# A planned kernel whose plan reckons loads at another rate, with one product issued in two pieces

## The chip, the cores and the metric

The kernel runs on one core of a Trainium2 chip. The core's engines work side by side, each through a list of instructions of its own, in order: TensorE (matrix products; PE in the profile, with its weight loads as PEld), VectorE (DVE), ScalarE (ACT), GpSimd (POOL) and SyncE (SP). In this kernel GpSimd does little but issue the loads from DRAM, and SyncE issues the transposes and the stores. An instruction that needs another engine's result waits for a semaphore, and everything behind it in its engine's list waits with it.

The metric is the time of one execution on the device in microseconds (us), as the median of several runs.

## The reference, cut to what matters

The inputs are u and v (8 sequences x 3072 tokens x 256), z (8 x 3072 x 64), and the weights w1, w2 (256 x 1024) and w_out (1024 x 256).

```python
scores = (1 / S) * z @ z.T            # per sequence, S = 3072
attn = max(scores, 0) ** 2
x = u * (attn @ v)                    # 24576 tokens x 256
h1, h2 = x @ w1, x @ w2
out = max(h1, h2) @ w_out
```

## The kernel before, in words

**The arithmetic.** max(h1, h2) is h2 + max(h1 - h2, 0). So the kernel forms w1 - w2 once, computes d = x (w1 - w2), takes its ReLU as g, and adds g @ w_out and x @ (w2 @ w_out). The product of w2 and w_out, called W2o, is made once, amid the first sequence: sixteen transposes of w2 on TensorE (job "w2t"), two copies of them out of PSUM to the tile w2T (jobs "w2T", 0 on VectorE and 1 on ScalarE), sixteen matrix products (job "w2o"), and two copies of the result to W2o_sb on ScalarE (jobs "w2o", 0 and 1). The two result tiles lie in two of the three pairs of PSUM banks that all score, d and output products share.

**Steps and groups.** A sequence has 24 blocks of 128 tokens, in six groups of four. A step works on one group of columns: 48 steps in all, six to a sequence. The score matrix is symmetric, so a tile of scores that one step has squared is transposed by a DMA (jobs "turn", issued by SyncE) and read again by a later step; a step's own diagonal tile is completed in the same way. The first three steps use plain products; the others use a seven-product scheme for 2 x 2 blocks, for which VectorE makes sums and differences of the score tiles (es), of the values v (the folds, lf) and of the accumulators (e). For each step TensorE does first products ("Xa", "Xb") and second products ("Ya", "Yb") into two accumulators, with the d products and output products of the steps before laid in between.

**The plan.** Nothing is scheduled by hand at the instruction level. The kernel declares jobs: what a job writes and reads, which jobs it needs, which engines can do it and at what reckoned cost. The order of TensorE is fixed by the list `work` (lines 1271 to 1380), into which the score tiles are laid. Then `find_orders` (line 1774) plays the jobs through, engine by engine: each engine takes, of the jobs that are ready by the reckoning, the one due first; ReLUs, squares and the like may go to ScalarE or VectorE. `find_dues` (line 1750) sets the due times from TensorE's list. `share_wide` (line 1851) gives the 19 wide buffers (score tiles, turned tiles, also w2 and w2T) to tiles by the reckoned end of their last use, and `share_mm` (line 1869) the pairs of PSUM banks. Up to 24 rounds are played, with a margin added to each job that TensorE had to wait for, and the round with the earliest reckoned end gives the order of every engine's list. On the chip only the lists, the buffers and the semaphores are left: the reckoned times are not enforced.

**How the plan reckons a DMA.** All DMAs of GpSimd and SyncE go through one line in `settle` (line 1789): `dma_free` is the time at which the line is free, and each DMA adds its own time, from the table `DMA`, times a factor: `DMA_FULL` = 1.1 for those that begin in the plan's first 100 us, `DMA_PART` = 0.9 later. SyncE also can't be more than 4.5 us ahead of that line (`DMA_AHEAD`). So in the plan a load makes the transposes behind it late, and the other way round. Loads that are timed start when TensorE reaches a given instruction (`load`, line 106).

Of the kernel before, what the change touches and what calls it, by code (L numbers as in the profile page):

```python
# [11 lines left out]
def kernel(  # L12
# [23 lines left out]
    B, S, D = u.shape  # L36
# [10 lines left out]
    KD = D // P  # L47
# [37 lines left out]
    def matmul(*args, **kw):  # L85
        newest[0] = pin(nc.tensor.matmul(*args, **kw)).ins  # L86
        for ins in fence:
            tc.add_manual_dep(newest[0], ins.name, SYNC, reason="a bank's other half of rows")
        fence.clear()
# [148 lines left out]
    def tile_of(pool, key):  # L238
        return bufs[pool, key].tile
# [1035 lines left out]
    def put(ns, shares, key, reads=()):  # L1275
        work.append((ns, shares, key, reads))
# [29 lines left out]
    for n, st in enumerate(steps):  # L1306
        if not st.plain:
            m = n - LAG + 1

            def d_part(part, i, m=m):  # L1310
                put(430, True, ("d" + part, m, i))

            def half(name, which, begin=lambda i: None, groups=slice(None)):
                for i, g in enumerate(st.groups[groups]):
                    begin(i)
                    put(
                        PE256 * (4 if which else 3),
                        False,
                        (name, n, g),
                        rows_read(st, g) if name == "Xa" else (),  # L1320
                    )

            seven = steps[n - LAG].seven

            def d_parts(names):
                for name in names.split():
                    d_part(name[0], int(name[1]))

            if n == LAG:
                put(900, True, ("w2t",))  # L1330
                put_d(0)
                half("Xa", 0, lambda i: put(1800, True, ("w2o",)) if i == W2O_AT else None)
            if seven:
                put_seven(n - LAG, 0)
                d_parts("a0")
                put_seven(n - LAG, 1)
                d_parts("b0")
            else:
                put_o(n - LAG)
            if n > LAG:  # L1340
                half("Xa", 0)
                if seven:
                    put_seven(n - LAG, 2)
                else:
                    d_parts("a0")
            half("Xb", 0)
            if seven:
                if n == LAG:
                    put_seven(n - LAG, 2)
                d_parts("a1 a2")  # L1350
                put_seven(n - LAG, 3)
                d_parts("b1 b2")
                half("Ya", 1, lambda i: d_parts("a3") if i == A3_AT else None)
            else:
                d_parts("b0 a1 a2 b1 b2 a3" if n > LAG else "a0 a1 b0 a2 b1 b2 a3")
                half("Ya", 1)
            d_parts("b3")
            half("Yb", 1)
            continue
        lat = LAT_OWN if n > LAG else 6 * 432  # L1360
        own = st.rows
        n_plain = 0

        def put_plain(ks, dcs, reads):
            global_i = len(plain_todo)
            i = sum(t[0] is st for t in plain_todo)
            plain_todo.append((st, i, ks, dcs))
            put(PE512 * len(ks) * len(dcs), False, ("plain", st.n, i), reads)

        for i, k0 in enumerate(own):  # L1370
            if i in ((0, 1) if n else ()) + (len(own) - 2, len(own) - 1):
                if i in (0, len(own) - 2):
                    ks = [own[i], own[i] + 1, own[i + 1], own[i + 1] + 1]
                    for dc in range(KD):
                        put_plain(ks, [dc], [((n, own[i]), lat), ((n, own[i + 1]), lat)])
                continue
            for k in (k0, k0 + 1):
                put_plain([k], range(KD), [((n, k0), lat)])
# [229 lines left out]
        after=at_step(0, 2, 6),  # L1608
    )

    def w2o_products(_):
        for dc in range(KD):
            ps = tile_of("mm", ("w2o", dc))
            for nb in range(KF):
                matmul(
                    ps[:, 0, :D],
                    tile_of(*W2T)[:, dc, nb, :],
                    w_out_sb[:, nb, :],
                    start=(nb == 0),
                    stop=(nb == KF - 1),  # L1620
                )

    job(
        ("w2o",),
        {"PE": 16 * PE256},
        w2o_products,
        deps=[("w2T", 0), ("w2T", 1), ("wo",)],
        new=[("mm", ("w2o", dc)) for dc in range(KD)],
        uses=[W2T],
        lag=150,  # L1630
    )
    for dc in range(KD):
        job(
            ("w2o", dc),
            {"ACT": 300},
            lambda eng, dc=dc: copy(eng, W2o_sb[:, dc, :], tile_of("mm", ("w2o", dc))[:, 0, :D]),
            deps=[("w2o",)],
            uses=[("mm", ("w2o", dc))],
            lag=200,
        )  # L1640
# [133 lines left out]
    def find_orders():  # L1774
        idle_from = {"PE": 0, "ACT": 900, "DVE": 1300, "SP": 0, "POOL": 0}
        ready = {e: [] for e in idle_from}
        emitted = []
        dma_free = [10000]

        def release(j):  # L1780
            at = 0
            for d in j.all_deps:
                at = max(at, d.done)
            for d in j.all_after:
                at = max(at, d.begin + 1)
            for e in j.ways:
                ready[e].append((at, j))

        def settle(j, begin, ns):
            j.begin, j.done = begin, begin + ns + j.lag  # L1790
            if j.key in FIRST_LOADS:
                j.done = FIRST_LOADS[j.key]
            elif j.dma:

                dma_free[0] = max(dma_free[0], begin + DMA_START["SP" if "SP" in j.ways else "POOL"]) + (DMA_FULL if begin < DMA_FULL_TO else DMA_PART) * j.dma
                j.done = dma_free[0] + DMA_END
                if "SP" in j.ways:
                    idle_from["SP"] = max(begin + SP_ISSUE, dma_free[0] - DMA_AHEAD)
            for nxt, _ in j.succ:
                nxt.waits -= 1  # L1800
                if not nxt.waits:
                    release(nxt)

        for j in list(jobs.values()):
            if not j.waits and j.key not in HEAD_JOBS:
                release(j)
        for key in [k for k in jobs if k in HEAD_JOBS]:
            settle(jobs[key], -1, 0)
            for e in jobs[key].ways:
                ready[e] = [r for r in ready[e] if r[1] is not jobs[key]]  # L1810


        def left_to_act(j, t):
            if j.key[0] not in ("relu", "g", "oc"):
                return False
            return max(t, idle_from["ACT"]) + j.ways["ACT"] <= max(t, idle_from["DVE"]) + j.ways["DVE"] + RELU_BIAS


        def left_to_dve(j, t):
            if j.key[0] != "square":  # L1820
                return False
            return max(t, idle_from["DVE"]) + j.ways["DVE"] <= max(t, idle_from["ACT"]) + j.ways["ACT"] + SQUARE_BIAS

        while len(emitted) < len(jobs) - len(HEAD_JOBS):
            best = None
            for e, todo in ready.items():
                if e == "DVE":
                    todo = [r for r in todo if not left_to_act(r[1], r[0])]
                if e == "ACT":
                    todo = [r for r in todo if not left_to_dve(r[1], r[0])]  # L1830
                if not todo:
                    continue
                found = [(max(t, idle_from[e]), j.due, j) for t, j in todo]
                at, _, j = min(found, key=lambda x: x[:2])

                if e != "PE":
                    near = [x for x in found if x[0] <= at + PATIENCE]
                    at, _, j = min(near, key=lambda x: x[1] + WAIT_COST * (x[0] - at))
                if best is None or at < best[0]:
                    best = at, e, j  # L1840
            assert best, [k for k, j in jobs.items() if j.begin is None][:20]
            at, e, j = best
            for o in j.ways:
                ready[o] = [r for r in ready[o] if r[1] is not j]
            idle_from[e] = at + (j.ways[e] if e != "POOL" else 1000)
            settle(j, at, j.ways[e])
            emitted.append((j, e))
        return emitted
# [149 lines left out]
```

## Time and profile before

| | us |
|---|---|
| median of 3 runs | 898.25 |
| lowest and highest of them | 895.57, 901.81 |
| the profiled execution | 892.38 |
| its span, first to last instruction | 890.3 |
| TensorE busy in the span | 883.2 |
| VectorE, ScalarE, GpSimd busy | 790.7, 757.8, 60.0 |

The profiled execution is one run of its own, so durations from it are set against 892.38, not against the median. A row of a group or of the timeline gives the start (in us from the span's start), the time taken, engine, line, operation and the tiles in the form out<-in; "x3" means three such instructions merged; what stands in brackets is the engine's idle time ahead of it and what ended it. A row of the windows gives, for a stretch, its length and then busy time and count of TensorE, its weight loads, VectorE, ScalarE and GpSimd, then the granted TensorE clock, the DMA engines' share and GB/s. A row of DMA issues ends with the us from issue to landing. Many operations of this kernel share a helper's line (L86 is every matrix product, L103 every DMA of SyncE, L107 every load), so tiles and order tell which is meant.

### The profile page before, as it was taken

What the parts mean: (1) busy time and instruction counts of PE and PEld (TensorE: products, weight loads), DVE (VectorE), ACT (ScalarE), POOL (GpSimd) and SP (SyncE); (2) the same over time, 40 slices, a digit from 0 to 9 for tenths busy, and PEclk for the clock granted to TensorE, in tenths of its full rate; (3) what the DMA queues carried; (4) which work ended last, traced back from release to release, by engine and by line L of the source; (5) the groups of instructions that cost most, each with busy time, mean ns of one, the idle gap of its engine ahead of it and who ended that gap; (6) DMA issues with size and microseconds to landing.
All of it is one profiled execution on the core that took longest, in us unless ns stands there. A gap on an engine that the chain in (4) does not pass through costs nothing.

```text
span 890.3 us, 37187 instructions
## 1 busy us (share of the span) xinstructions
PE 883.2 (99%) x16349; PEld 736.2 (83%) x16349; DVE 790.7 (89%) x1698; ACT 757.8 (85%) x951; POOL 60.0 (7%) x127
## 2 busy tenths in 40 slices
PE   9999999999999999999999999999999999999998
PEld 3368888888889988888888888889888888888885
DVE  6877799999999999999998999999998999999970
ACT  8867997899978999789997899978999799987635
POOL 3100000000000000000000000000000000000000
PEclk9999999999999999999999999999999999999999
DMA  9999999999999969999799997999999999896711
GB/s 156 170 169 151 192 208 177 184 179 162 175 168 192 195 118 173 178 188 186 124 177 176 187 177 133 168 188 195 154 142 178 182 201 158 150 186 116 132 50 72
DMA packets 380851, 146.13 MB, mean 164 GB/s; under 512 B 359184, under 2 KB 360848, under 8 KB 380688
## 3 DMA queue, kind: packets, MB, share of 16 engines
q1 hardware_dynamic: 364128, 114.01, 78.0%
q0 software_dynamic: 16560, 29.74, 23.4%
q8 instruction: 127, 2.08, 0.9%
q14 instruction: 36, 0.29, 0.1%
HBM read 59.77 MB, written 25.17 MB: 95 GB/s over the span
## 4 chain that ended last, share of the span: by engine, by line
PE 93%; ACT 3%; DVE 2%; issue 1%; DMA 1%; POOL 0%; POOLq 0%; ACTq 0%
PE acc L86 48%; PE s_ps L86 45%; ACT a_sb L282 2%; ACT g_sb L282 1%; DVE gs L296 1%; DMA z_sb<-in_z_dram 1%; DVE e L299 0%; DVE e L296 0%; ACT o_sb L282 0%; ACT a_sb L288 0%; PE tpz_c L129 0%; ACT w2T_sb L293 0%; PE w2t_ps L1588 0%; DVE a_sb L290 0%; DVE w2T_sb L293 0%
## 5 line engine op out<-in xcount | busy, mean ns | idle before, releaser
L86 PEld LDWEIGHTS <-v_sb 64*128 64x128 bf16 (+1 forms) x4464 | 334.2, 94 | 65.2 <-issue 7.0
L282 ACT ACTIVATE a_sb<-s_ps 128x1024 bf16<-128x1024 f32 (+1 forms) x335 | 302.3, 940 | 30.9 <-PE s_ps L86 27.8
L86 PEld LDWEIGHTS <-lf 64*128 64x128 bf16 x3240 | 264.6, 94 | 15.3 <-POOLq L94 3.2
L86 PE MATMUL acc<-es,v_sb 64*128 64x256 bf16 x2160 | 275.9, 269 | 0.1
L86 PE MATMUL acc<-es,lf 64*128 64x256 bf16 x1080 | 245.2, 269 | 0.1
L86 PE MATMUL acc<-a_sb,lf 64*128 64x256 bf16 x1224 | 233.2, 269 | 0.0
L86 PE MATMUL s_ps<-xT,w_sb 64*128 64x512 bf16 (+1 forms) x1484 | 213.9, 376 | 0.1
L288 ACT ACTIVATE a_sb<-a_sb 128x1024 bf16<-128x1024 bf16 (+1 forms) x223 | 210.0, 967 | 1.5
L282 ACT ACTIVATE g_sb<-s_ps 128x1024 bf16<-128x1024 f32 x187 | 185.5, 1021 | 20.0 <-PE s_ps L86 17.6
L86 PE MATMUL acc<-aT,lf 64*128 64x256 bf16 x936 | 177.5, 269 | 0.0
L86 PE MATMUL acc<-a_sb,v_sb 64*128 64x256 bf16 (+1 forms) x1344 | 141.9, 279 | 0.7 <-issue 0.4
L86 PE MATMUL s_ps<-zT 64*128 64x512 bf16 (+2 forms) x774 | 121.8, 334 | 0.8 <-DVE zT L130 0.2
L296 DVE TENSOR_TENSOR es<-aT 128x1536 bf16<-128x1536 bf16 (+1 forms) x117 | 106.3, 930 | 0.6
L86 PEld LDWEIGHTS <-gs 64*128 64x128 bf16 x2688 | 98.2, 94 | 9.4
L86 PEld LDWEIGHTS <-w_sb 64*128 64x128 bf16 (+1 forms) x1488 | 79.4, 94 | 27.0 <-issue 1.2
L86 PEld LDWEIGHTS <-g_sb 64*128 64x128 bf16 x2336 | 91.0, 94 | 10.8 <-POOLq L94 7.1
L290 DVE TENSOR_TENSOR a_sb<-a_sb 128x1024 bf16<-128x1024 bf16 (+1 forms) x113 | 73.0, 649 | 28.3 <-ACT a_sb L282 28.1
L299 DVE TENSOR_TENSOR es<-a_sb 128x512 bf16<-128x512 bf16 x198 | 78.6, 418 | 9.4 <-PE acc L86 9.3
L86 PE MATMUL acc<-aT,v_sb 64*128 64x256 bf16 x936 | 86.8, 269 | 0.0
L86 PE MATMUL s_ps<-wf_sb,gs 64*128 64x128 bf16 x2016 | 81.0, 216 | 0.0
L86 PE MATMUL s_ps<-w_out_sb,g_sb 64*128 64x128 bf16 (+1 forms) x1664 | 79.1, 226 | 0.0
L296 DVE TENSOR_TENSOR es<-a_sb 128x1024 bf16<-128x1024 bf16 x108 | 72.9, 682 | 0.0
(92 smaller groups left out, 1086.2 us busy)
## 6 DMA issues: line engine op xcount, KB each, us to landing
out_dram<-o_sb SPq DMA_DIRECT2D x47, 512.0 KB, 4.5
v_sb<-in_v_dram POOLq DMA_DIRECT2D x48, 256.0 KB, 5.7
u_sb<-in_u_dram POOLq DMA_DIRECT2D x48, 256.0 KB, 5.2
aT<-a_sb SPq DMA_TRANSPOSE x228, 5.1
z_sb<-in_z_dram POOLq DMA_DIRECT2D x7, 384.0 KB, 6.5
w_sb<-in_moe_w_dram POOLq DMA_DIRECT2D x2, 512.0 KB, 6.3
uT<-u_sb SPq DMA_TRANSPOSE x48, 5.4
a_sb<-a_sb SPq DMA_TRANSPOSE x45, 5.5
```

The costliest lines, as they stand in the source:

```text
L86: newest[0] = pin(nc.tensor.matmul(*args, **kw)).ins
L282: pin(nc.scalar.activation(out_ap, in_ap, AF.Relu))
L288: pin(nc.scalar.activation(ap, ap, AF.Square))
L290: pin(nc.vector.tensor_mul(ap, ap, ap))
L296: pin(nc.vector.tensor_add(*args))
L299: pin(nc.vector.tensor_sub(*args))
```

## The change

Two things are changed. First, the job "w2o" of sixteen products becomes two jobs "w2op" of eight, one for each half of w2T; each needs only its own half and takes one result tile, and each copy of the result needs only its own job. They follow each other in `work` where the one job stood. Second, in `settle`, a DMA of GpSimd (a load) that begins between 18 and 100 us of the plan adds 0.5 of its time to the line in place of 1.1. No load is moved by hand, and no instruction is added or taken away; the orders of VectorE, ScalarE and SyncE and the wide buffers come out of the plan anew.

```diff
-                half("Xa", 0, lambda i: put(1800, True, ("w2o",)) if i == W2O_AT else None)
+                half("Xa", 0, lambda i: [put(900, True, ("w2op", dc)) for dc in range(KD)] if i == W2O_AT else None)
...
-    def w2o_products(_):
-        for dc in range(KD):
-            ps = tile_of("mm", ("w2o", dc))
-            for nb in range(KF):
-                matmul(
...
-    job(
-        ("w2o",),
-        {"PE": 16 * PE256},
-        w2o_products,
-        deps=[("w2T", 0), ("w2T", 1), ("wo",)],
-        new=[("mm", ("w2o", dc)) for dc in range(KD)],
-        uses=[W2T],
-        lag=150,
-    )
+    def w2o_products(dc):
+        ps = tile_of("mm", ("w2o", dc))
+        for nb in range(KF):
+            matmul(
...
     for dc in range(KD):
+        job(
+            ("w2op", dc),
+            {"PE": 8 * PE256},
+            lambda _, dc=dc: w2o_products(dc),
+            deps=[("w2T", dc), ("wo",)],
+            new=("mm", ("w2o", dc)),
+            uses=[W2T],
+            lag=150,
+        )
         job(
             ("w2o", dc),
             {"ACT": 300},
             lambda eng, dc=dc: copy(eng, W2o_sb[:, dc, :], tile_of("mm", ("w2o", dc))[:, 0, :D]),
-            deps=[("w2o",)],
+            deps=[("w2op", dc)],
...
-                dma_free[0] = max(dma_free[0], begin + DMA_START["SP" if "SP" in j.ways else "POOL"]) + (DMA_FULL if begin < DMA_FULL_TO else DMA_PART) * j.dma
+                dma_free[0] = max(dma_free[0], begin + DMA_START["SP" if "SP" in j.ways else "POOL"]) + (0.5 if 18000 < begin < 100000 and "POOL" in j.ways else DMA_FULL if begin < DMA_FULL_TO else DMA_PART) * j.dma
```

More of the change, by code (lines that the diff above doesn't have):

```diff
@@ L1609 @@
     )
-    def w2o_products(_):
-        for dc in range(KD):
-            ps = tile_of("mm", ("w2o", dc))
-            for nb in range(KF):
-                matmul(
[L1616 to L1620, printed above, removed]
-                )
-    job(
-        ("w2o",),
-        {"PE": 16 * PE256},
-        w2o_products,
-        deps=[("w2T", 0), ("w2T", 1), ("wo",)],
-        new=[("mm", ("w2o", dc)) for dc in range(KD)],
-        uses=[W2T],
-        lag=150,
-    )
-    for dc in range(KD):
+    def w2o_products(dc):
+        ps = tile_of("mm", ("w2o", dc))
+        for nb in range(KF):
+            matmul(
+                ps[:, 0, :D],
+                tile_of(*W2T)[:, dc, nb, :],
+                w_out_sb[:, nb, :],
+                start=(nb == 0),
+                stop=(nb == KF - 1),
+            )
+    for dc in range(KD):
+        job(
[6 more added lines that the diff above has]
+            lag=150,
+        )
         job(
```

## The prediction

> **What bounds the kernel now.** I read the page first (busy shares, the chain that ended last), then the busy time by stretches, then the order of time around the two places that the diff names.
>
> ```profile
> span 890.3 us, 37187 instructions
> PE 883.2 (99%) x16349; PEld 736.2 (83%) x16349; DVE 790.7 (89%) x1698; ACT 757.8 (85%) x951; POOL 60.0 (7%) x127
> PE 93%; ACT 3%; DVE 2%; issue 1%; DMA 1%; POOL 0%; POOLq 0%; ACTq 0%
> ```
>
> ```profile
> 0.00:10.00 10.00, 7.97 (x48) 3.28 (x49) 4.44 (x8) 6.15 (x7) 5.25 (x16) 1.00 0.81 143
> 110.00:120.00 10.00, 10.00 (x214) 8.71 (x211) 9.63 (x22) 9.63 (x12) 0.53 (x1) 1.00 1.08 208
> 200.00:300.00 100.00, 99.91 (x2001) 88.67 (x1997) 94.30 (x203) 89.77 (x113) 6.26 (x14) 1.00 1.09 178
> 300.00:400.00 100.00, 99.80 (x1956) 87.78 (x1952) 93.90 (x207) 89.38 (x113) 6.42 (x14) 1.00 1.06 166
> 400.00:500.00 100.00, 99.49 (x1990) 85.06 (x1988) 93.67 (x204) 89.47 (x114) 6.61 (x14) 1.00 1.09 172
> 500.00:600.00 100.00, 99.91 (x1962) 83.01 (x1960) 93.82 (x205) 90.54 (x113) 6.07 (x13) 1.00 1.07 165
> 600.00:700.00 100.00, 99.91 (x2009) 87.24 (x2005) 94.77 (x204) 89.20 (x114) 6.61 (x14) 1.00 1.09 170
> 700.00:800.00 100.00, 99.91 (x1969) 86.93 (x1967) 93.80 (x206) 92.60 (x116) 5.84 (x11) 1.00 1.04 173
> 850.00:892.00 42.00, 36.84 (x570) 28.40 (x564) 14.79 (x29) 17.06 (x25) 0.00 (x0) 0.98 0.14 52
> ```
>
> TensorE (the first pair of columns after the length) sets the end: 93% of the chain, and idle 890.3 - 883.2 = 7.1 us in all. Of these about 2.0 lie in the first 10 us, 3.5 after 850 (40.3 us of span are left there), and the six stretches of 100 us from 200 to 800 add only 0.09 + 0.20 + 0.51 + 0.09 + 0.09 + 0.09 = 1.1. The change touches neither the first 10 us nor the end. So nothing that it does can save more than some 2 us, but whatever newly holds TensorE is lost in full, since no later stretch has room to give it back. That asymmetry carries the forecast. The granted clock is 1.00 in each of these stretches up to 800.
>
> **The change part by part.** *The split of the product.* The list of TensorE is, instruction for instruction, the same in both kernels: the sixteen products of w2 and w_out stay in one run at the same place. The trace shows what they wait for now.
>
> ```profile
> 51.98 3.94 PE L86 MATMUL s_ps<-xT,w_sb 128*128 128x512 bf16 x16
> 52.18 0.69 DVE L293 COPY w2T_sb<-w2t_ps 128x1024 bf16<-128x1024 bf16 x1 [0.16 <-PE w2t_ps L1588]
> 52.90 1.01 ACT L293 COPY w2T_sb<-w2t_ps 128x1024 bf16<-128x1024 bf16 x1 [0.80 <-DVE w2T_sb L293]
> 53.81 3.78 ACT L282 ACTIVATE g_sb<-s_ps 128x1024 bf16<-128x1024 f32 x4
> 55.81 1.95 PE L86 MATMUL s_ps<-w_out_sb,w2T_sb 128*128 128x256 bf16 x16
> 57.44 0.73 ACT L293 CAST W2o_sb<-s_ps 128x256 bf16<-128x256 f32 x2
> ```
>
> The first copy of W2o begins at 57.44, before the sixteenth product ends at 55.81 + 1.95 = 57.76: the two halves are already released apart, because waits hang on instructions and not on the plan's jobs. The split is worth 0 in execution; it only takes a wait out of the plan's reckoning. If I am wrong here, the most it can save is what is lost around it: sixteen products at the 0.109 us which the plan gives one (16 x 0.109 = 1.74) against 1.95, so 0.2 us.
>
> *The rate of the loads.* It takes no work away: the same loads, transposes, squares and sums, in another order on VectorE, ScalarE and SyncE, and with other buffers for the wide tiles. In the built program three moves matter.
>
> (a) SyncE. The transposes of step 1's second half and of step 0's last group move ahead of those of step 2.
>
> ```profile
> 30.13 3.90 SPq L103 DMA_TRANSPOSE aT<-o_sb  x1
> 34.15 1.37 SPq L103 DMA_TRANSPOSE uT<-u_sb  x1
> ...
> 40.07 4.57 SPq L103 DMA_TRANSPOSE aT<-a_sb  x2
> ...
> 41.90 2.74 SPq L103 DMA_TRANSPOSE aT<-a_sb  x1
> ...
> 46.85 1.21 SPq L103 DMA_TRANSPOSE a_sb<-a_sb  x1
> ```
>
> The rows from 40.07 and from 41.90 are the same list asked from later on: they show that step 2's pair goes out at 40.07 and 41.90. From 34.15 to the next issue is 1.4 us. In the changed list five transposes stand between the one issued at 30.13 (done with issuing at 34.0) and step 2's pair, where there were two. At 1.4 us each they end at 41.0, so the pair goes out at about 41.0 and 42.4. They fill SyncE's wait for step 2's squares, from 36.9 to 40.07, and from 50 to 100 us SyncE runs ahead of where it was. TensorE was not waiting there, so this alone saves nothing.
>
> (b) The first copy of w2T. Its buffer is now the one that held step 2's scores for group 3, which the pair of step 2 reads; so this copy on VectorE waits for their landing, where before it waited for TensorE and VectorE alone. The view of DMA issues, asked for a tenth of a us around each, gives the us to landing of the first of the pair, then of w_out and the second, then of the transpose issued at 46.85; its last two rows are the packets of the loads' queue and of the transposes' queue from 46 to 47 us:
>
> ```profile
> aT<-a_sb SPq DMA_TRANSPOSE x1, 3.4
> ...
> w_out_sb<-in_moe_w_out_dram POOLq DMA_DIRECT2D x1, 512.0 KB, 8.9
> aT<-a_sb SPq DMA_TRANSPOSE x1, 11.0
> ...
> a_sb<-a_sb SPq DMA_TRANSPOSE x1, 10.2
> ...
> q0 software_dynamic: 240, 0.12, 88.5%
> q1 hardware_dynamic: 239, 0.06, 46.3%
> ```
>
> The second lands at 41.9 + 11.0 = 52.9. The copy began at 52.18. With the landing where it is, the copy is 0.7 us late; with the second issued 0.5 us later, 1.2. Behind it stand the ScalarE copy of the other half (52.90, already waiting for it), then the four ReLUs that free PSUM for the d products and for the split product: TensorE's third d product starts at the end of the copy, and each later one at the end of a ReLU. So the delay passes to TensorE whole. Bounds: 0 (if the pair lands by 52.2, which takes 10.3 us in place of 11.0) and 5 (if both of the pair are caught among the loads: the transpose issued at 46.85, next in the queue after the one that took 11.0, landed at 57.0, which is 4.1 later). I take 1.25, near the row of 11.0.
>
> The Trainium skill (DMA: Bandwidth & Descriptors, section Queues, rings and completion order) says that each DMA engine takes turns between its queues, a packet from each. The 240 and 239 packets from 46 to 47 us agree. By that rule a transpose that is queued beside a load pays for it nearly packet by packet, which speaks against reckoning a load at half for what stands behind it; by it the sum would keep 1.25 for one transpose caught and about 5 for two.
>
> (c) The first fold of the last pair of value groups for sequence 1. In VectorE's new list it stands right behind the squares of step 6, ahead of the two gs sums and the sums that free the accumulators; before, it stood behind them. Its load is the first row here, with its us to landing in the second; the third is the quickest load of that size in this stretch, one of u.
>
> ```profile
> 107.32 0.53 POOL L107 DMA_DIRECT2D v_sb<-in_v_dram  x1 [4.22 <-PE acc L86]
> ...
> v_sb<-in_v_dram POOLq DMA_DIRECT2D x1, 256.0 KB, 6.0
> ...
> u_sb<-in_u_dram POOLq DMA_DIRECT2D x1, 256.0 KB, 4.2
> ```
>
> ```profile
> 110.90 0.42 DVE L299 TENSOR_TENSOR es<-a_sb 128x512 bf16<-128x512 bf16 x1
> 112.91 1.22 DVE L296 TENSOR_TENSOR gs<-g_sb,gs 128x2048 bf16<-128x2048 bf16 x1
> 115.15 0.42 DVE L296 TENSOR_TENSOR e<-e,acc 128x256 f32<-128x256 f32 x1
> 115.49 0.42 DVE L296 TENSOR_TENSOR lf<-v_sb 128x512 bf16<-128x512 bf16 x1
> ```
>
> The squares end at 110.9, the load lands at 113.3 (6.0) or 111.5 (4.2): VectorE, which takes its list in order, stands still for 0.6 to 2.4 us. On the other side the 1.13 us of the wide gs sum (112.91 to 114.04) now comes after the accumulators' sums, so their last, at 115.15, is 1.1 - 0.3 = 0.8 earlier but for the stall: TensorE's next product into the accumulators waits for it 0 to 1.6 us. VectorE is 96% busy there (9.63 of 10), so the rest is given back slowly and reaches later products. I take 0.6, with bounds 0 and 2.4; a shorter queue after (a) speaks for the low half.
>
> (d) From the second sequence on the lists differ by exchanged neighbours alone. Bound: the 1.1 us of the six stretches, to gain or to lose; no row decides between them, and I take half of the gain, -0.5, because the 0.09 that recurs in five of the six stretches looks like one wait per sequence that another order may meet or miss.
>
> Sum: 0 + 0 + 1.25 + 0.6 - 0.5 = +1.35 us on the profiled execution's 892.38 us (span 890.3 and 2.1 around it), so 893.7. That execution is 5.9 below the median shown, 898.25, and 3.2 below the lowest; the sum goes on the median: **899.6**.
>
> **The rivals.**
> 1. *Two transposes caught.* If step 2's pair both meet the load of w_out, (b) costs 1.25 + 4.1 = 5.35: the sum is 5.45, the time 903.7. For it: five transposes at 1.4 us leave no idle time ahead of 41 us. Against: the one issued at 40.07 met no load and landed in 3.4.
> 2. *Faster, by a slack regained.* The last transpose for step 5's last group, its us to landing, and the product that reads it:
>
> ```profile
> 93.26 3.93 SPq L103 DMA_TRANSPOSE aT<-a_sb  x1
> ...
> aT<-a_sb SPq DMA_TRANSPOSE x1, 7.3
> ...
> 100.77 0.29 PE L86 MATMUL acc<-aT,v_sb 64*128 64x256 bf16 x2
> ```
>
> It lands at 100.6, and the product starts at 100.8. In (a) it goes out some 5 to 10 us earlier. If the runs that lie 3.2 to 9.4 above the profiled one lose part of that where such a landing is late, the new order gives some back: half of the 5.9, so 898.25 - 2.95 = 895.3. It decides as soon as a landing there is more than 0.2 us later than in this trace. Against: this trace shows no TensorE idle time there, so I can't see that the other runs lose it there.
> 3. *Nothing changes.* The pair lands by 52.2 and the fold's load in 4.2 us: 0 + 0.6 - 0.5, time 898.3.
>
> **How the numbers follow.** Forecast 0.50 (its own range 897 to 902.5: the bounds 0.7 to 2 of (b), 0 to 2.4 of (c), -1.1 to 1.1 of (d)), rival 1 0.20, rival 2 0.20, rival 3 0.10. The range goes from rival 2 with the same 2 us that runs scatter, 893.5, to rival 1 with the upper half of (c), 905.5. What a measurement of this kernel can tell from no change is about 1%, 9 us. All four cases lie within it; beyond it would be rival 1 with all upper bounds, 5 + 2.4 + 1.1 = 8.5, and another wait of that kind that I did not find (0.06), or rival 2 with more than the whole 5.9 (0.03). So 0.03 faster, 0.91 same, 0.06 slower.
>
> **What would show it.** Right: VectorE's first w2T copy released by a transpose's landing and about 1 us later behind the transposes of w2; the chain of waits still TensorE at over 90%; a gap on VectorE ahead of the lf fold near 111 us, released by the v load; the transposes of step 5 landed well before 95 us. Wrong: a new idle stretch of TensorE of more than 3 us anywhere (a buffer handed on too early that I did not find), or a busy sum of TensorE that changes though its list does not.

## The result, and the profile after

The changed kernel takes 903.75 us (median of 12 runs, 898.54 to 909.36), the kernel before 896.8 us beside it (12 runs, 892.2 to 903.75): a ratio of 1.008, with a 95% interval of 1.0053 to 1.0107. So it is slower by some 7 us, within the 1% that the prediction called no change. The predicted 899.6 is 4 us too low; the rival with both transposes caught had said 903.7. A median counts every run; a ratio counts only runs within 1.5% of the fastest of their kernel, so it need not be the quotient of two medians.

The profiled execution of the changed kernel took 905.27 us, 1.5 over its median, and that of the kernel before 892.38, 4.4 under the median here. So of the 12.9 us between the two traces only 7.0 are the change's; the traces show where it can lie, the medians how much it is. First the page of the changed kernel: span, busy shares, and the shares of the chain that ended last.

```profile
span 903.5 us, 37204 instructions
PE 887.1 (98%) x16349; PEld 737.5 (82%) x16349; DVE 790.6 (88%) x1697; ACT 758.9 (84%) x952; POOL 59.8 (7%) x127
PE 87%; DMA 5%; DVE 4%; ACT 3%; issue 1%; POOL 0%; DVEq 0%; ACTq 0%; POOLq 0%
```

TensorE's busy sum rose by only 3.9 us (883.2 to 887.1) with the same 16349 products; its idle time rose from 7.1 to 16.4. In the chain DMA went from 1% to 5%: transfers now hold the path. The windows say where. First two of the kernel before, then those of the changed one:

```profile
50.00:60.00 10.00, 9.90 (x98) 6.46 (x98) 9.58 (x22) 7.34 (x10) 0.53 (x1) 1.00 1.21 151
120.00:135.00 15.00, 15.00 (x294) 13.05 (x291) 14.39 (x35) 14.90 (x19) 0.21 (x1) 1.00 1.20 198
```

```profile
50.00:60.00 10.00, 7.25 (x40) 3.51 (x38) 5.00 (x11) 5.84 (x7) 0.00 (x0) 0.83 1.28 98
120.00:135.00 15.00, 12.27 (x228) 10.29 (x226) 14.97 (x38) 12.96 (x16) 0.53 (x1) 1.00 1.10 146
200.00:300.00 100.00, 99.83 (x1951) 88.54 (x1948) 93.79 (x207) 89.17 (x113) 6.05 (x13) 1.00 1.09 167
300.00:400.00 100.00, 99.72 (x1989) 87.32 (x1986) 94.11 (x206) 89.64 (x114) 6.58 (x14) 1.00 1.08 167
400.00:500.00 100.00, 97.29 (x1876) 80.17 (x1874) 90.80 (x199) 85.78 (x108) 6.05 (x13) 0.98 1.07 162
500.00:600.00 100.00, 99.93 (x2000) 83.01 (x1998) 93.41 (x200) 90.40 (x114) 6.57 (x14) 1.00 1.05 170
600.00:700.00 100.00, 99.08 (x1941) 85.70 (x1938) 94.27 (x207) 91.37 (x116) 6.59 (x14) 1.00 1.13 167
700.00:800.00 100.00, 99.92 (x2001) 87.48 (x1999) 94.68 (x203) 89.00 (x113) 6.35 (x12) 1.00 1.08 173
```

TensorE stood idle for 2.75 us between 50 and 60 (with the granted clock at 0.83), 2.73 between 120 and 135, and 2.71 between 400 and 500. The first two lie exactly where the prediction put steps (b) and (c). Here is the first of them, VectorE, ScalarE and then TensorE, with one step of the chain ahead of it (its second number is the time from the transpose's issue to its landing):

```profile
42.59 11.79 DMA aT<-a_sb
```

```profile
54.51 0.69 DVE L293 COPY w2T_sb<-w2t_ps 128x1024 bf16<-128x1024 bf16 x1 [2.81 <-DMA aT<-a_sb]
55.23 1.01 ACT L293 COPY w2T_sb<-w2t_ps 128x1024 bf16<-128x1024 bf16 x1 [3.45 <-DVE w2T_sb L293]
51.65 1.89 PE L86 MATMUL s_ps<-xT,w_sb 128*128 128x512 bf16 x8
56.30 3.35 PE L86 MATMUL s_ps<-xT,w_sb 128*128 128x512 bf16 x8 [2.75 <-ACT w2T_sb L293]
59.44 2.17 PE L86 MATMUL s_ps<-w_out_sb,w2T_sb 128*128 128x256 bf16 x16
```

The second transpose of step 2's pair is issued at 42.59 and under way for 11.79 us. VectorE's first w2T copy waits for it (2.81 us), ScalarE's for VectorE's, TensorE's third d product for ScalarE's (2.75 us). Then TensorE pays a second time. Its next eight matrix instructions take 3.35 us, where sixteen of the same kind took 3.94 in the trace of before (1.97 for eight), and the sixteen of w2T take 2.17 in place of 1.95. The windows of 2 us from 56 on give the granted clock, in the third column from the end:

```profile
56.00:58.00 2.00, 1.71 (x5) 0.65 (x5) 1.81 (x5) 2.00 (x4) 0.00 (x0) 0.64 1.32 105
58.00:60.00 2.00, 2.00 (x7) 0.89 (x6) 0.00 (x0) 1.32 (x3) 0.00 (x0) 0.51 1.31 103
60.00:62.00 2.00, 2.00 (x25) 1.60 (x25) 0.72 (x3) 1.43 (x3) 0.00 (x0) 1.00 1.37 204
```

From the first d product to the last product of w2T, TensorE needs 9.96 us (51.65 to 61.61), against 5.78 before (51.98 to 57.76). So one wait of 2.75 us cost some 4.2 us, of which the slower clock is 1.4. The Trainium skill (TensorE: Matmul & The Clock Gate, Part 1) says that the clock falls to half after an idle window of about 3.4 us and comes back after as long a busy one; the 0.51 agrees, the length doesn't: here 2.75 us of idle time was enough.

The second place: the wait of the fold on VectorE, and then TensorE's waits from 108 to 135 us (total, times, longest).

```profile
118.28 0.43 DVE L296 TENSOR_TENSOR lf<-v_sb 128x512 bf16<-128x512 bf16 x1 [2.73 <-DMA v_sb<-in_v_dram]
```

```profile
PE acc L86 <- DVE e L296: 1.7, 1, 1.7
PE acc L86 <- DVE e L299: 1.0, 1, 1.0
```

VectorE stands 2.73 us for the load of v, and the sums behind the fold, which free the accumulators, hold TensorE for 1.7 and 1.0 us. Together with the 4.2 that is 6.9 us at the two places, as much as the medians differ. That one execution comes out so even is partly luck: the experiments show that the first place's part varies. Nothing in the runs ties the rest of this trace's loss to the change; its largest piece, near 420 us, comes last in this text.

### The profile page after: what moved, and what is told of

Same layout as the page of the kernel before. It is cut to its first block, busy times and chain, and to the rows that moved or that the text cites. A ratio compares the mean times of both kernels' runs of the same rounds, so it can differ in the third digit from the quotient of the medians.

```text
span 903.5 us, 37204 instructions
## 1 busy us (share of the span) xinstructions
PE 887.1 (98%) x16349; PEld 737.5 (82%) x16349; DVE 790.6 (88%) x1697; ACT 758.9 (84%) x952; POOL 59.8 (7%) x127
## 4 chain that ended last, share of the span: by engine, by line
PE 87%; DMA 5%; DVE 4%; ACT 3%; issue 1%; POOL 0%; DVEq 0%; ACTq 0%; POOLq 0%
PE acc L86 44%; PE s_ps L86 43%; DMA v_sb<-in_v_dram 3%; ACT a_sb L282 1%; DMA aT<-a_sb 1%; ACT g_sb L282 1%; DVE es L296 1%; DMA z_sb<-in_z_dram 1%; DVE es L299 1%; DVE a_sb L290 0%; DVE gs L299 0%; DVE gs L296 0%; DVE e L299 0%; DVE e L296 0%; DVE xT L303 0%
## 5 line engine op out<-in xcount | busy, mean ns | idle before, releaser
L86 PE MATMUL s_ps<-xT,w_sb 64*128 64x512 bf16 (+1 forms) x1484 | 216.7, 378 | 2.8 <-ACT w2T_sb L293 2.8
```

## The experiments

The questions: do the two waits carry the 7 us, does the split or SyncE's order carry some of it, and do the two prices add up? The edits are made on the finished plan, so that no order moves but the one named. Ratios are to the kernel before, run beside each (medians 897.04 beside e1 to e4, 897.8 beside e5 to e8, 896.16 beside e9 to e12).

| kernel | SyncE's order | w2T waits for the pair | fold | median, us | ratio (95%) |
|---|---|---|---|---|---|
| changed | new | yes | early | 903.75 | 1.0080 (1.0053 to 1.0107) |
| e1 | new | no | early | 903.6 | 1.0061 (1.0026 to 1.0095) |
| e2 | new | yes | late | 904.93 | 1.0091 (1.0058 to 1.0124) |
| e12, e2 again | new | yes | late | 905.32 | 1.0094 (1.0068 to 1.0119) |
| e3 | new | no | late | 897.34 | 0.9995 (0.9969 to 1.0022) |
| e4, split alone | nearly old | no | late | 895.8 | 0.9984 (0.9957 to 1.0010) |
| e5 | old | yes | late | 896.81 | 1.0001 (0.9973 to 1.0030) |
| e6 | old | no | early | 900.54 | 1.0040 (1.0014 to 1.0065) |
| e7 | old | yes | early | 900.82 | 1.0055 (1.0022 to 1.0087) |
| e8, rate alone | new | yes | early | 904.7 | 1.0077 (1.0048 to 1.0105) |
| e9 | three transposes behind the pair | yes | late | 903.43 | 1.0073 (1.0041 to 1.0104) |
| e10 | new | no | early, its load sooner | 899.26 | 1.0014 (0.9982 to 1.0047) |
| e11 | three transposes behind the pair | yes | early, its load sooner | 902.6 | 1.0061 (1.0031 to 1.0091) |

### Undoing the two places in the changed kernel (e1, e2, e3), and the split alone (e4)

The edit of e1, just ahead of where the buffers are made; the later tiles of two wide buffers change places, and w2T gets w2's buffer as before:

```diff
+    first, second = bufs["T", "w2"].slot, bufs["A", (2, 3)].slot
+    later = [use for use in best_slots if use[0] in ("A", "T") and use not in (("T", "w2"), ("A", (2, 3)))]
+    for use in later:
+        if use in taker and bufs[use].slot in (first, second) and taker[use].begin > 40000:
+            bufs[use].slot = first + second - bufs[use].slot
```

> The changed kernel, with only the two wide buffers exchanged: w2T gets w2's buffer again, as before, and the later score tiles of step 4 get the other one. All orders stay. Theory T (most of the 6.9 us between the medians is held at two places, some 4 us at the first w2T copy, the slower clock behind it counted in, and some 3 us at the fold ahead of step 6): the w2T copy is released by TensorE and begins near 52 us, the 2.75 us hold of TensorE at 56 us falls to below 0.7, the clock there stays at 1.00, and the kernel takes about 4 us less than the changed one, some 3 us (0.3%) more than the kernel before. Rival D (the DMA line around 40 to 100 us is crowded and something else is caught in its place): another hold of over 2 us between 45 and 100 us, and the ratio to before stays at 1.006 to 1.010. Rival R (the difference lies mostly in random holds of instruction supply): ratio within 1.006 to 1.010 without any hold that has an end in a semaphore.

The edit of e2, ahead of the loop that issues the jobs; e3 has both edits:

```diff
+    moved = [x for x in emitted if x[0].key == ("fold", 1, 2, 0)][0]
+    emitted.remove(moved)
+    emitted.insert([x[0].key for x in emitted].index(("ye", 5)) + 1, moved)
```

> The changed kernel with one item of VectorE's list moved: the lf fold of sequence 1's last pair of value groups stands behind the sums that free step 5's accumulators, as before. Theory T: no 2.7 us stall of VectorE near 118 us, the holds of TensorE between 118 and 128 us fall from 3.1 us to below 0.7; about 3 us less than the changed kernel, some 4 us (0.4%) more than before; the hold at 56 us stays. Rival D: the v load is late for whatever reads it next, so a hold of 1.5 us or more shows up within the next 15 us, and the ratio stays at 1.006 or more. Rival R: ratio stays at 1.006 to 1.010 with no hold there.

> Both of these at once: buffers exchanged and the fold behind the accumulators' sums; what is left of the change are the split product, SyncE's order and the exchanged neighbours in VectorE's and ScalarE's lists. Theory T: within 1.5 us of the kernel before, ratio 0.998 to 1.002. Rival D: 3 us or more above before (1.0035 and up). Rival S (the later sequences, which lose 0.14 in place of 0.19 us each of TensorE's time, are really better): 0.3 us below before, which no timing here can tell from nothing, so only the windows after 200 us can show it.

The edit of e4, the changed kernel with the old rate:

```diff
-(0.5 if 18000 < begin < 100000 and "POOL" in j.ways else DMA_FULL if begin < DMA_FULL_TO else DMA_PART) * j.dma
+(DMA_FULL if begin < DMA_FULL_TO else DMA_PART) * j.dma
```

> The split of the product alone: loads amid the first sequence reckoned at 1.1 as before, two jobs of eight products. The wide buffers come out as before, and the fold stays where it was. Theory T: ratio 0.998 to 1.002 to the kernel before; the w2T copy is released by TensorE. Rival P (the two pieces cost by themselves, through the PSUM pairs that the two results take): a hold of 1 us or more at the products of w2 and w_out, ratio 1.002 or more.

Measured: with both places undone nothing of the loss is left (e3, 0.9995), so no more than some 2 us can lie in the split, SyncE's order and the exchanged neighbours by themselves. The split alone costs nothing (e4, 0.9984), and its w2T copy is released by TensorE, as expected:

```profile
DVE w2T_sb L293 <- PE w2t_ps L1588: 0.2, 1, 0.2
```

But the one-sided repairs did not gain what theory T expected, 4 us for e1 and 3 for e2. e2 is clearly against it: T's 1.004 lies outside its interval. e1's 1.0061 is higher than T's 1.003 too, but its interval reaches down to 1.0026, so e1 alone does not refute T. In e1 the w2T copy did begin without the wait, but TensorE was held at the fold (1.1 and 1.0 us; VectorE waited 2.1 for the load) and for 1.1 us by the transpose of step 3's diagonal tile. In e2 the fold's part shrank (VectorE still waited 1.0 us for the load, and TensorE 1.5 near 126 us), but the hold at w2T stayed, with 1.5 us in this one execution. TensorE's waits in e1 from 110 to 130 us and, last, from 45 to 135, then VectorE's from 50 to 60 in e2:

```profile
PE acc L86 <- DVE e L296: 1.1, 1, 1.1
PE acc L86 <- DVE e L299: 1.0, 1, 1.0
...
PE acc L86 <- DMA a_sb<-a_sb: 1.1, 1, 1.1
```

```profile
DVE es L299 <- DMA a_sb<-a_sb: 3.3, 1, 3.3
DVE w2T_sb L293 <- DMA aT<-a_sb: 1.5, 1, 1.5
```

1.5 us don't explain 8. But the profiled execution of e2 took 899.67, 5.3 under the median of e2, so it says little of the others. Either the hold at w2T is longer in most executions, or something else holds e2. So I asked next whether the wait costs anything without SyncE's new order.

### Adding the two places to the kernel before (e5, e6, e7), and the rate alone (e8)

The edits are those of e1 and e2, made in the kernel before; there the exchange of buffers gives w2T the buffer that waits, and the fold goes behind the last squares of step 6, `("square", 6, 22)`. e8 is the kernel before with the new line in `settle` and the product in one job.

> The kernel before, with only the two wide buffers exchanged, so that the first w2T copy waits for step 2's pair of transposes; every order stays. So far each of the two edits alone, undone in the changed kernel, left it 5 to 8 us above before, and both undone left nothing. Theory A (each has its own price, adding up to 7): 3 to 4 us above before. Theory I (either is enough: one hold at either place costs nearly all of it, and the second little more): 5 to 8 us above. Theory O (SyncE's order, five transposes ahead of the pair, is needed for the pair to be late enough): within 2 us of before, since here the pair goes out at 40 and 42 us as it did; the w2T copy then begins at most 1 us later.

> The kernel before, with only the lf fold of sequence 1's last value groups moved ahead of the sums that free step 5's accumulators. Theory A: about 3 us above before, VectorE standing 2 to 3 us ahead of the fold, released by the v load. Theory I: 5 to 8 us above. Theory O: as A at most; less (0 to 1) if the v load lands by 112 us as it did in the profile of before.

> The kernel before with both edits added: buffers exchanged and the fold early. What it lacks of the change are the split, SyncE's order and the exchanged neighbours. Theory A and theory I: 5.5 to 8.5 us above before, as the changed kernel. Theory O: clearly less, 0 to 3.

> The kernel before with the other rate alone and the product in one piece; the plan gives it the changed kernel's wide buffers (the w2T copy waits for step 2's pair), and the fold early. All theories on the two places: 5 to 9 us above before, as the changed kernel. If the split is what makes the rate's order costly: within 2 us of before.

e5 decides it: the same wait at w2T, with SyncE's old order, costs nothing that can be told (1.0001), as theory O expected. With the fold late, the four cases are old order without and with the wait (1 and 1.0001) and new order without and with it (0.9995 in e3, 1.0091 in e2): only the two together cost. e8 shows that the rate alone, with the product in one piece, brings the whole loss (1.0077). VectorE's wait from 50 to 60 us in e5, then over 45 to 135 us in e8:

```profile
DVE w2T_sb L293 <- DMA aT<-a_sb: 0.3, 1, 0.3
```

```profile
DVE w2T_sb L293 <- DMA aT<-a_sb: 5.7, 1, 5.7
```

The same wait: 0.3 us behind the old order, 5.7 behind the new one. Why, the transposes' own queue shows: its packets, their MB and the time they took as a share of 16 engines (packets that overlap can bring it above 100%), from 38 to 40 and from 40 to 42 us, first in the kernel before, then in the changed one.

```profile
q1 hardware_dynamic: 156, 0.03, 8.1%
q1 hardware_dynamic: 599, 0.15, 38.8%
```

```profile
q1 hardware_dynamic: 1541, 0.38, 97.2%
q1 hardware_dynamic: 1497, 0.38, 125.8%
```

In the kernel before, the queue was nearly empty when the pair came, and the first of the pair landed in 3.4 us, ahead of the loads. In the changed one, the three transposes moved ahead fill it; the pair, issued at 41.1 and 42.6, stands behind them, and the load of w_out is issued just ahead of both, at 41.03, where in the kernel before it came between the two, at 41.30. The copy waits for the second of the pair. That one took 11.0 us in the kernel before and 11.8 in the changed one, so the lateness is made of small pieces: 0.7 us that it would have been late in the old order, 0.7 from the issue (42.59 for 41.90) and 0.8 from the landing. Over the traces the pieces grow: the second lands at 52.0 to 52.9 us with the old order (before, e5, e7), and at 53.1, 54.4, 57.4 and 59.0 with the new order and the wait (e2, changed, e8, e12). In e8 the landing itself took 14.5 us; in e12 the transpose goes out only at 50.97, since one ahead of the pair took 6.43 us to issue and the first of the pair 5.11. With the old order SyncE stands idle for 2.8 to 3.2 us ahead of the pair (before, e5, e7), which can take up such a delay; with the new one it goes from one transpose straight to the next. That is how two steps that the prediction priced each for itself depend on each other: SyncE's order sets when the pair lands, and the buffer makes TensorE wait for it.

The fold early, in the old order, costs some 3.6 us by the ratio and 2.7 by the medians (e6), as theory A had it. In its trace VectorE waits 2.5 us for the load, and TensorE 2.9 for the sums. After that hold, too, the clock halves; TensorE's wait and the windows from 118 on:

```profile
PE acc L86 <- DVE e L296: 2.9, 1, 2.9
```

```profile
118.00:120.00 2.00, 0.86 (x8) 0.66 (x9) 1.93 (x6) 0.00 (x0) 0.00 (x0) 0.79 1.03 195
120.00:122.00 2.00, 2.00 (x18) 1.36 (x16) 2.00 (x5) 1.02 (x1) 0.53 (x1) 0.50 0.89 170
```

e7, both edits in the old order, came out at 1.0055, between the theories: the fold's price, and 1.3 us of waiting at w2T in its trace.

### Taking away what the waits wait for (e9, e10, e11), and e2 once more (e12)

The edits, with remarks added that say where a line belongs: e9 is e2 with the transposes of step 1's second half and step 0's last group behind the pair; e10 is e1 with the fold's load right behind the load before it; e11 is the changed kernel with both.

```diff
+    def later(key, behind):
+        moved = [x for x in emitted if x[0].key == key][0]
+        emitted.remove(moved)
+        emitted.insert([x[0].key for x in emitted].index(behind) + 1, moved)
+    for key in (("turn", 0, 22), ("turn", 0, 20), ("turn", 1, 18)):   # e9, e11
+        later(key, ("turn", 2, 14))
+    later(("v", 1, 0), ("v", 1, 5))                                   # e10, e11
```

> The changed kernel with the fold back behind the sums, and with three transposes (step 1's last, and the two of step 0's last group) moved in SyncE's list from ahead of step 2's pair to behind it, about as before; w2T stays in the buffer that waits for the pair. Theory O (the wait at w2T is dear only because SyncE's new order sends the pair out beside the load of w_out): the pair goes out near 38 and 40 us and lands by 53, the hold at the w2T copy is below 1.5 us, the kernel within 2.5 us of before (ratio below 1.003), and 4 us or more under the one with the fold alone put back. Rival W (the wait itself, wherever the pair stands): a hold of 1.5 to 6 us at the copy, ratio 1.005 to 1.009.

> The changed kernel with the two wide buffers exchanged, the fold left early, and the load that it reads started about 5 us sooner, right behind the load before it. Theory T (the early fold costs because its load lands after the squares): no wait of VectorE on that load, no hold of TensorE over 0.7 us between 115 and 130 us, 3 to 5 us under the one with the buffers alone exchanged, within 2 us of before. Rival F (the fold's place is not it, and the rest is in SyncE's order): ratio 1.004 or more, with a hold behind a transpose between 55 and 105 us.

> The changed kernel with both waits left in its lists, but with what they wait for made early: the three transposes behind step 2's pair, and the fold's load some 5 us sooner. Theories O and T together: ratio 0.998 to 1.003, so the change's cost would be the two arrivals and nothing else. If buffers or the fold's place cost by themselves: 1.005 or more.

> The changed kernel with the fold alone put back, once more, beside the kernels it is to be compared with. Two places with prices of their own (4 at w2T, 3 at the fold): 3 to 5 us above before. A price at w2T that varies with the landing of the pair and is more than 4 on average: 6 to 9 above, as at the first time; the hold at the w2T copy in this profile differs from the 1.6 us of the first by more than 1 us.

e10 went as theory T expected: with its load some 5 us sooner, the early fold waits for nothing, TensorE isn't held between 110 and 130 us, and the kernel can't be told from before (1.0014). So by the trace the fold's price is the lateness of its load, not its place; the ratios of e1 and e10 point the same way, though their intervals overlap.

e12 confirmed e2 (1.0094) and showed why its first profile looked too cheap: this time the copy waited 6.3 us, and the clock halved during the hold itself.

```profile
DVE w2T_sb L293 <- DMA aT<-a_sb: 6.3, 1, 6.3
```

```profile
54.00:56.00 2.00, 0.57 (x3) 0.17 (x2) 0.00 (x0) 0.00 (x0) 0.00 (x0) 1.00 1.26 101
56.00:58.00 2.00, 0.00 (x0) 0.00 (x0) 0.00 (x0) 0.00 (x0) 0.00 (x0) 0.72 1.13 191
58.00:60.00 2.00, 0.00 (x0) 0.00 (x0) 0.93 (x2) 0.20 (x1) 0.00 (x0) 0.50 1.26 277
```

TensorE's hold at w2T in the new order was 2.75, 1.48, 5.65 and 6.29 us in the four executions profiled (changed, e2, e8, e12), a mean of 4.0. With the slower clock, the stretch from the first d product to the last of w2T is longer than the 5.78 us of before by 4.2, 1.4, 8.2 and 7.4 us, a mean of 5.3. It is a price drawn anew in every execution.

e9 and e11 missed. I had expected the pair to go out near 38 and 40 us and the loss to go. SyncE's issues in e9, and then in e11, from the transpose ahead of the pair on (the first of each "x3" is the first of the pair; a row's time is the whole run of issues):

```profile
34.46 6.12 SPq L103 DMA_TRANSPOSE aT<-a_sb  x1
40.69 1.25 SPq L103 DMA_TRANSPOSE uT<-u_sb  x1
42.72 8.68 SPq L103 DMA_TRANSPOSE aT<-a_sb  x3
```

```profile
39.73 5.08 SPq L103 DMA_TRANSPOSE aT<-a_sb  x3
44.87 9.20 SPq L103 DMA_TRANSPOSE aT<-o_sb  x2
54.16 5.56 SPq L103 DMA_TRANSPOSE aT<-a_sb  x1
59.83 1.23 SPq L103 DMA_TRANSPOSE a_sb<-a_sb  x1
```

In e9's execution one issue ahead of the pair took 6.12 us, so the pair went out at 42.7 after all and the copy waited 4.2 us. In e11's, the pair went out at 39.73 and the w2T copy waited for nothing on SyncE; but now the transpose of step 3's diagonal tile, which the kernel before issues at 46.85, came at 59.83, behind the three, and TensorE waited for that (its waits from 55 to 70 us):

```profile
PE acc L86 <- DMA a_sb<-a_sb: 5.2, 1, 5.2
```

So moving the three behind the pair isn't the old order: there they stand behind the diagonal's transpose too. The same hold is in the traces of e3 (2.5 us), e10 (1.2) and e1 (1.1), the kernels with the new order and no wait at w2T. In the traces with the old order (before, e5 to e7) TensorE waits from 45 to 135 us for no transpose longer than 0.6 us, the wait at w2T apart. So each of the other orders made some reader late; which one, the order decided.

What stays open: the prices don't add up. With the new order, the two places cost 1.0080 together, where the one-sided kernels gave 1.0061 and 1.0091 to 1.0094. And e2's and e12's 8 us and more are above the mean of 5.3 that four traces show at w2T. The traces do fit their own executions: e1's took 899.39 us, 2.4 above the median beside it, and shows holds of 1.1, 1.0 and 1.1; e12's took 903.45, 7.3 above, and lost 7.4 at w2T. But one trace per kernel doesn't give its median. The intervals are up to 0.7% wide; whether the two prices overlap, other waits join in, or the scatter does it, the runs can't tell. That a shorter landing at w2T would by itself repair the new order wasn't shown, since in e9 the pair was late all the same. No kernel tried is faster than the kernel before by more than can be told.

## Why the prediction was right or wrong

**What bounds the kernel** held: no run won anything, and what newly held TensorE at the two places was not given back later.

**The split, 0**: right (e4, and e8 without it).

**(a) SyncE, 0 by itself**: right in price to within some 2 us (e3, 0.9995), right in the issue times of the pair (41.0 and 42.4 forecast, 41.11 and 42.59 in the trace), wrong in what follows. SyncE was to run ahead from 50 to 100 us, with step 5's transposes landed well before 95. By the clock it was later: the u transpose that went out at 51.59 now does at 59.59, and the last of step 5's at 95.46 in place of 93.26. TensorE was later by more, though: its product that reads this last one starts at 105.26 in place of 100.77.

```profile
59.59 1.30 SPq L103 DMA_TRANSPOSE uT<-u_sb  x1
95.46 1.67 SPq L103 DMA_TRANSPOSE aT<-a_sb  x1
...
105.26 0.47 PE L86 MATMUL acc<-aT,v_sb 64*128 64x256 bf16 x4
```

So the landing, at 95.46 + 8.9 = 104.4 us, is 0.9 us ahead of its reader, where it had been 0.2 ahead. What the new order makes late is the pair and the diagonal's transpose: I counted the five transposes at 1.4 us each as issues and left out that each also fills the queue in front of the pair, in the very 2 us before the load of w_out starts.

**(b) the w2T copy, 1.25 with bounds of 0 and 5**: the mechanism, place and releaser were right, and this is the term that was mis-sized. I moved the pair 0.5 us later (it was 0.7) and kept its landing time of 11.0; the trace has 11.79 and a copy 2.3 us later than before, other executions up to 6.3 of waiting. Added to that is what I had no term for, the half clock after the hold (1.4 us here). In this execution that makes 4.2 us; the price over many runs, with the new order and the fold late, is 8 us or a little more (e2 and e12 against e3), above my upper bound of 5. The rival with both transposes caught, 5.45 us and 903.7, described this better than the forecast, and it had a chance of only 0.20 (the first of the pair did take 8.1 us to land, in place of 3.4): I argued against it from a transpose that had met an empty queue, though step (a) fills that queue.

**(c) the fold, 0.6 with bounds of 0 and 2.4**: again the right mechanism and too small a size. The stall of VectorE was 2.73 us, over the bound of 2.4: the load was issued at 111.88, as the row shows, and the fold that waited for it began 6.4 us later, at 118.28.

```profile
111.88 0.53 POOL L107 DMA_DIRECT2D v_sb<-in_v_dram  x1 [4.22 <-PE acc L86]
```

I had let a shorter queue after (a) speak for the low half, and the queue wasn't shorter. Nor did the wide gs sum's move give back 0.8: TensorE lost 2.73. Alone in the old order it is some 3.6 us by the ratio (e6), the half clock included.

**(d) the later sequences, -0.5**: not seen. The six stretches from 200 to 800 us lose 0.17 + 0.28 + 2.71 + 0.07 + 0.92 + 0.08 = 4.2 us in place of 1.1, of which 2.1 are one hold without a releaser near 420 us and 0.8 one wait for VectorE near 650; e3, with nearly the same lists there, is level with before. If the order gave the half microsecond, it is too small to tell.

**The rivals.** "Faster" was wrong: against its reader that landing came 0.7 us earlier, and no run won anything by it. "Nothing changes" needed a pair landed by 52.2 and a load in 4.2 us; neither came. The sum's 1.35 against 7 is thus two terms of the right kind, each taken far too small. The prediction took the landing times of one execution, a quick one, as if they were properties of the kernel.

**The range, and luck.** The forecast's own range, 897 to 902.5, does not follow from the bounds named with it: they add up to -0.4 and +5.5, which on 898.25 gives 897.9 to 903.8. The measured 903.75 is outside the range as written and at the very top of the one that the bounds give; the wide range, 893.5 to 905.5, holds it only by the part that rival 1 added. (Likewise 895.3 less 2 is 893.3 and not 893.5.) The base helped as well: 898.25 was the median of 3 runs, and 12 runs give 896.8. So rival 1's 903.7 meets the measured time partly by luck, with 5.45 us forecast on the higher base against 7 measured on the lower, and the forecast's 1.35 is 5.6 us too small, more than the 4 us between 899.6 and 903.75.

## What to carry to other kernels

When a change moves transfers forward in a queue, price what then stands behind them at the time when the next large load starts, not only the issue slots; and price a buffer's new reader together with that order, since the same wait cost nothing that could be told behind one order and 8 us behind another. Where a kernel is bound by TensorE, add the clock's part to a hold of more than some 2 us (1.4 us at the hold of 2.75 here). A wait for a transfer is a distribution: one trace gives one draw of it (here 1.5 to 6.3 us for the same wait), and the bounds have to be wider than that draw.

## What the runs showed of the hardware

*The clock after a hold.* Between 10 and 850 us, holds of TensorE of up to 1.81 us left the granted clock at 1.00 (1.21 in e7, 1.48 and 1.81 in e2, 1.7 in the changed kernel); holds of 2.11 and 2.75 (changed kernel), 2.51 (e3), 2.92 (e6), 2.95 (e7), 4.10 (e9), 5.16 (e11), 5.65 (e8) and 6.29 us (e12) halved it. By the windows it stayed low for 3.3 to 3.5 us after the five holds under 3 us, and for 6.7 to 6.9 us, at times from within the hold on, at the four longer ones. The one of 2.11 is near 420 us in the changed kernel; TensorE's row, and the two windows behind it:

```profile
421.24 0.23 PE L86 MATMUL s_ps<-wf_sb,gs 64*128 64x128 bf16 x2 [2.11 <-issue]
```

```profile
421.00:423.00 2.00, 1.76 (x16) 0.92 (x18) 0.96 (x3) 1.32 (x3) 0.00 (x0) 0.70 1.24 207
423.00:425.00 2.00, 2.00 (x21) 1.26 (x18) 1.89 (x6) 0.99 (x2) 0.53 (x1) 0.50 1.63 220
```

*Holds without a releaser.* That hold ended with nothing that the profile shows ("issue"), in the middle of a run of output products, and cost nearly as much again by the clock. e8 has one of 1.64 us near the same place, e10 and e11 have 1.2 and 1.1, the others none of over 1 us there; e2 has one of 1.81 near 742 us. Its cause wasn't tested.

*Transposes beside loads.* The two transposes of step 2's pair, alike in shape, took 3.4 us from issue to landing (the first, into a nearly empty queue) and 11.0 us (the second, beside the load of w_out) in the kernel before, and 8.1 and 11.8 us in the changed one, with others ahead and the load beside. The Trainium skill (DMA: Bandwidth & Descriptors, Queues, rings and completion order) has the engines take turns between queues packet by packet. One for one is what the two queues show from 46 to 47 us in the kernel before (240 and 239 packets) and from 45 to 46 us in the changed one (196 of the loads, 195 of the transposes), but not from 46 to 47 us there (300 and 118, with three transposes under way). So equal turns alone don't give a landing time; how much of it is the load and how much the queue's own packets was not separated.
